# A recurrent-memory transformer with mixers on one Trainium2 core: the last mixer chunk in another order, with unread matmuls in its waits

## Chip, cores and metric

The kernel runs on one core of a Trainium2 chip, in one launch. The metric is the device time of that launch in microseconds (us); lower is better.

## What is computed

Four layers in a row on x of 2048 rows by 640: attention with a recurrent memory (A), a mixer with an MLP (B), and both again with the same weights. Cut to what matters:

```python
# A: 64 segments of 32 rows; 8 memory rows go in front of each and come out of it
for s in range(n_seg):
    h = concatenate([mem, x[s*32:(s+1)*32]])               # 40 rows
    q, k, v = h @ Wq, h @ Wk, h @ Wv                       # 32 heads of 192
    p = softmax(where(mask, q @ k.T * scale, -1e9))
    o = (p @ v) @ Wo
    mem, out = o[:8], o[8:]
# B
h = gelu(layernorm(x) @ w1)
h = concat(h[:, 0:160] one row later, h[:, 160:320] one row earlier,
           h[:, 320:480] two rows later, h[:, 480:640] two rows earlier)
x1 = x + h @ w2
return x1 + gelu(layernorm(x1) @ w3) @ w4
# all
x = x + A(layernorm(x)); x = x + B(layernorm(x)); x = x + A(layernorm(x)); x = x + B(layernorm(x))
```

## The kernel before

**Two lanes.** The first A layer and the second run side by side as two lanes, the second five segments behind the first (`LAG`). `attention_step(t)` does segment t of lane 0 and segment t - 5 of lane 1 in one go, with both lanes' 40 rows side by side (`N` is 80 columns, or 40 where only one lane has a segment: the first five steps and the last five). There are 69 steps. The 32 heads are eight groups of four; for each pair of groups `proj_pair` multiplies with Wk, Wq and Wv, partly from weights that stay in SBUF and partly from a ring of eight streamed tiles (`wst`), and `attend` does scores, softmax, values and Wo for one group. The result goes to `yTB` (L696).

**Chunks.** The mixer runs on 64 rows of both lanes at a time: `chunk(c)` and `chunk_end(c)`. Every second step carries one chunk among its matmuls, from its own ring (`wstB`) and its own two psum banks (pool B). `chunk` transposes `yTB` back to rows (psx), adds the residual (L847, xw), takes the layer norm (`ln_ops`, `apply_ln`; the inverse root is a `pow` on GpSimd, L721), transposes the result (psv), copies it to SBUF (`vT`, L896) and multiplies with w1 (L918). Because the mixer needs rows that come later, there is a look-ahead: a second row tile `lnx` with four rows beyond the chunk and the first layer norm's rows for coming segments. It has its own transposes (psl), add (L851), statistics (L874), root (L881), normalisation (L887, which writes into the same buffer `vb` as the chunk's own, so that the transposes of `vb` come after it) and copy (L900). `gelu` is four operations: square on ScalarE, polynomial on VectorE, tanh on ScalarE, product on VectorE, here in up to nine pieces because the four column quarters are shifted by one or two rows (L765). Then w2 (L963), a residual add (L969), a layer norm, w3 in three parts of five, five and two blocks of 128 columns (L998), GELU, and in `chunk_end` w4 (L1024), the last add (L1030) and the store (L1042), which GpSimd issues.

**The last chunk.** The last of 34 chunks, `last`, has only rows of lane 1 and comes after the last step, with nothing beside it. It puts its two halves of rows into the two lanes' places, so the rows at the seam are copied inside `hTB` by seven small VectorE copies (L947). Its psum tiles come from pool A's six banks, its GELU buffers lie over the resident Wv (`own`), and its weights were loaded during the last step over weights that are no longer needed (`homes`).

**What sets the order.** Nothing is issued as written. Every operation is given to a planner with an engine, an estimated length, a due time and the buffers that it reads and writes (`add`); `Plan.place` then runs a list schedule: of the operations that could start about now on an engine, the one with the earliest due time. The queues of the engines are issued in that order; a load that the planner held back for its pace gets a wait on an earlier matmul (`paced`, L1119 to L1125). So a changed estimate can change the order elsewhere. The due times of the last chunk are squeezed by `LAST_PACE`:

```python
        D = lambda x: base + x * STEP * (LAST_PACE if last else 1.0)
        PB = "A" if last else "B"
```

Of the kernel before, what the change touches and what calls it, by code (L numbers as in the profile page):

```python
# [21 lines left out]
HG = 4  # L22
# [7 lines left out]
OT_BUFS = 8  # L30
LAT = 0.12
# [39 lines left out]
class Op:  # L71
    __slots__ = ("e", "d", "due", "fn", "n", "succ", "ready", "slots", "start", "end", "dma", "i", "margin",
                 "paced", "last")


class Plan:
# [8 lines left out]
    def add(self, e, d, due, fn, r=(), w=(), a=(), dma=0, queue=None, margin=0.0):  # L85
# [6 lines left out]
        preds = set()  # L92
# [31 lines left out]
    def place(self):  # L124
# [27 lines left out]
        def est(o, t):  # L152
            s = max(t, o.ready)
            need = {}
            for b in o.slots:
                if b.slot is None:
                    need[b.cls] = need.get(b.cls, 0) + 1
            for c, n in need.items():
                fs = self.free_slots[c]
                if len(fs) < n:  # L160
                    return None
                s = max(s, fs[n - 1][0])
            if o.e == "SP":
                s = max(s, srv - ahead(o))
            return s
# [6 lines left out]
        while left:  # L172
# [29 lines left out]
            o.paced = e == "SP" and s <= srv - ahead(o) + 1e-9  # L202
# [38 lines left out]
def kernel(  # L241
# [87 lines left out]
    mask_b = ctile([L1, L1], bf16, "mask_b")  # L329
    nc.gpsimd.memset(mask_b[:], 0.0)  # L330
    keep(mask_b, L1, M, L1, -M, 1, -1, NEG)
    keep(mask_b, L1, M, L1, -M, 1, 0, 0.0)
# [11 lines left out]
    qT = qTw[:].rearrange("p (c n) -> p c n", c=GC)  # L344
    vFw = ctile([P, GC * NS], bf16, "vF")
    vF = vFw[:].rearrange("p (c n) -> p c n", c=GC)
    kT = [ctile([P, 8, NS], bf16, f"kT{i}") for i in range(2)]
    Vt = [ctile([NS, 2 * VP], bf16, f"V{i}") for i in range(2)]
# [23 lines left out]
    for i in range(2):  # L372
        nc.gpsimd.memset(kT[i][:], 0.0)
    for i in range(2):
        nc.vector.memset(Vt[i][:], 0.0)
    nc.gpsimd.memset(yTB[:], 0.0)
    nc.vector.memset(qTw[:], 0.0)
    nc.vector.memset(vFw[:], 0.0)
    nc.vector.memset(Pmw[:], 0.0)
# [131 lines left out]
    def attention_step(t):  # L511
# [4 lines left out]
        maskt = mask2[:] if both else (mask_a if 0 in ln else mask_b[:])  # L516
# [8 lines left out]
        def proj_pair(pr):  # L525
            s0 = base + sl * 2 * pr
            for kind, off in (("k", 0.0), ("q", 0.2), ("v", 0.5)):
                wbs, wv = load_pair(kind, pr, s0 + off * 2 * sl, LEAD_A)
                for j in range(2):
                    g = 2 * pr + j  # L530
                    G = t * NG + g
                    due = s0 + (off + 0.1 * j) * 2 * sl
# [3 lines left out]
                    for kcs in [range(0, nres)] + [range(kc, kc + 1) for kc in range(nres, KC)]:  # L536
                        def fn(op, pq=pq, wv=wv, j=j, kcs=kcs):
                            o = T(pq)
                            for cc in range(GC):
                                for kc in kcs:  # L540
                                    nc.tensor.matmul(out=o[:, cc, 0:N],  # L541
                                                     lhsT=wv(kc, GW * j + cc * P, GW * j + (cc + 1) * P),
                                                     rhs=h[:, kc, c0:c0 + N], start=(kc == 0 and cc == 0),
                                                     stop=(kc == KC - 1), skip_group_check=True)
                        wb = wbs[0] if kcs[0] == 0 else wbs[1 + kcs[0] - nres]
                        add("PE", mm_us(N, k=GC * len(kcs)), due + 0.01 * kcs[0], fn, r=(wb, *hk), a=(pq,))
                    if kind == "q":
                        q = qT

                        def fq(op, pq=pq, q=q):  # L550
                            nc.scalar.copy(out=q[:, :, 0:N], in_=T(pq)[:, :, 0:N])  # L551
                        add("ACT", act_us(GC * N), due, fq, r=(pq,), w=(B("qT"),))
                    elif kind == "k":
                        k_ = kT[G % 2]

                        def fk(op, pq=pq, k_=k_):
                            p4 = T(pq)[:].rearrange("p (h c) n -> p h c n", h=2)
                            k4 = k_[:].rearrange("p (h c) n -> p h c n", h=2)
                            nc.vector.tensor_copy(out=k4[:, :, 0::3, 0:N], in_=p4[:, :, 0::2, 0:N])  # L559
                        add("DVE", dve_us(4 * N), due, fk, r=(pq,), w=(B("kT", G % 2, 0),))  # L560
                        for part, (r0, r1, jj) in enumerate(((0, 64, 1), (64, P, 2))):
                            def fk2(op, pq=pq, k_=k_, r0=r0, r1=r1, jj=jj):
                                p4 = T(pq)[:].rearrange("p (h c) n -> p h c n", h=2)
                                k4 = k_[:].rearrange("p (h c) n -> p h c n", h=2)
                                nc.vector.tensor_copy(out=k4[r0:r1, :, jj, 0:N], in_=p4[r0:r1, :, 1, 0:N])  # L565
                            add("DVE", dve_us(2 * N), due, fk2, r=(pq,), w=(B("kT", G % 2, 1 + part),))
                    else:
                        vf, V_ = vF, Vt[G % 2]

                        def fvf(op, pq=pq, vf=vf):  # L570
                            nc.scalar.copy(out=vf[:, :, 0:N], in_=T(pq)[:, :, 0:N])  # L571
# [3 lines left out]
                        def fvt(op, pvt=pvt, vf=vf):  # L575
# [6 lines left out]
                        for hf in range(2):  # L582
                            def fe(op, pvt=pvt, V_=V_, hf=hf):
                                src = T(pvt)[0:N, GWH * hf:GWH * (hf + 1)].rearrange("n (a b) -> n a b", a=2)
                                v0 = hf * (VP - 64)
                                dst = V_[0:N, v0:v0 + 512].rearrange("n (a b) -> n a b", a=2)[:, :, 64 * hf:64 * hf + Dh]
# [5 lines left out]
                                w=(B("V", G % 2, hf),))  # L592

        def attend(g):
            G = t * NG + g
            s0 = base + sl * g
            q, k_, V_ = qT, kT[G % 2], Vt[G % 2]
# [3 lines left out]
            def fs(op):  # L601
                o = T(pss)
                seq = [(0, 1, 0, 0), (1, 1, 2, 3), (2, 1, 3, 4), (3, 1, 5, 7), (0, 2, 1, 1), (2, 2, 4, 5)]
                for n_, (i, w_, c, j) in enumerate(seq):
                    m_ = wide(c, GC - 1)
                    nc.tensor.matmul(out=o[0:m_, i * N:(i + w_) * N].rearrange("p (a b) -> p a b", a=w_),  # L606
                                     lhsT=qTw[:, c * NS:c * NS + m_], rhs=k_[:, j:j + w_, 0:N],
                                     start=(n_ == 0), stop=(n_ == len(seq) - 1), skip_group_check=True)
            add("PE", mm_us(N, N, 4) + mm_us(2 * N, N, 2), hi - 4, fs,
                r=(B("qT"), B("kT", G % 2, 0), B("kT", G % 2, 1), B("kT", G % 2, 2)), w=(pss,))  # L610
# [4 lines left out]
            def f1(op):  # L615
                o = T(pss)[0:N, 0:HG * N].rearrange("p (a b) -> p a b", a=HG)
                nc.vector.tensor_tensor_reduce(out=o, in0=o, in1=maskt.unsqueeze(1).to_broadcast([N, HG, N]),  # L617
                                               scale=-scale, scalar=3.0e38, op0=ALU.add, op1=ALU.min,
                                               accum_out=sm_[0:N, 0:1])
            add("DVE", dve_us(HG * N) + 0.02, hi - 4, f1, r=(pss,), w=(pss, smk))  # L620

            def f2(op):
                o = T(pss)[0:N, 0:HG * N].rearrange("p (a b) -> p a b", a=HG)
                nc.scalar.activation(out=Pb[0:N, :, 0:N], in_=o, func=ACT.Exp, bias=sm_[0:N, 0:1], scale=-1.0)  # L624
            add("ACT", act_us(HG * N) + 0.09, hi - 4, f2, r=(pss, smk), w=(Pk,))

            def f3(op):
                nc.vector.tensor_reduce(out=sm_[0:N, 2:2 + HG], in_=Pb[0:N, :, 0:N], axis=AX.X, op=ALU.add)  # L628
                nc.vector.reciprocal(out=sm_[0:N, 6:6 + HG], in_=sm_[0:N, 2:2 + HG])
                nc.vector.tensor_tensor(out=Pb[0:N, :, 0:N], in0=Pb[0:N, :, 0:N],  # L630
                                        in1=sm_[0:N, 6:6 + HG].unsqueeze(2).to_broadcast([N, HG, N]), op=ALU.mult)
# [529 lines left out]
```

## Time and profile before

| | |
|---|---|
| three runs, us | 3530.97, 3534.40, 3536.71; median 3534.4 |
| profiled execution, us | 3528.87, of which the profile's span 3527.2 |
| mean granted TensorE clock | 0.98 |
| busy: TensorE / VectorE / ScalarE / GpSimd | 94% / 70% / 43% / 7% |

By stretches of the span (start and end in us; in each row, after the length, the busy time of TensorE, of its weight loads, of VectorE, ScalarE and GpSimd, with the number of instructions; then the granted TensorE clock, the share of the DMA engines' time, and GB/s):

```profile
0.00:56.00 56.00, 35.17 (x750) 31.32 (x751) 19.74 (x79) 13.04 (x37) 6.85 (x23) 1.00 0.99 373
```
```profile
290.00:3261.00 2971.00, 2895.40 (x72649) 2832.60 (x72646) 2192.79 (x6399) 1349.38 (x3079) 215.00 (x416) 1.00 0.89 306
```
```profile
3483.80:3527.20 43.40, 17.00 (x144) 13.38 (x144) 17.07 (x54) 6.90 (x17) 3.62 (x6) 0.65 0.18 58
```

The first row is the opening, which loads the weights; the second the steps with two lanes; the third the last chunk. A row's busy time is read against its length: an engine near the length is a bound of that stretch, and where none is near, a chain of waits across engines sets the time. The granted clock is the share of TensorE's full speed that the hardware allowed; the records have it at 1.0 or 0.5, so a mean between them says for how long it was halved.

### The profile page before, as it was taken

The page shows a single profiled execution, that of the slowest core. Times are in us where ns is not written, and L with a number is a line of the kernel's source. Part 1 is how long each engine was busy: PE and PEld are TensorE (multiplying, and loading weights), DVE is VectorE, ACT ScalarE, POOL GpSimd, SP SyncE. Part 2 cuts the span into 40 slices and gives each one's busy share as a digit, 9 for nine tenths or more (in the row PEclk, how much of TensorE's full clock was granted, in tenths as well). Part 3 has the DMA queues.
Part 4 walks back from the last instruction along what each step waited for, and adds up shares of the span by engine and source line. Part 5 has one row for each costly group of instructions (what it writes and reads, how often), then busy time and mean ns, then how long its engine had stood idle before and what let it go on. Part 6 is the DMA issues. An engine that isn't in the chain of part 4 may idle for free.

```text
span 3527.2 us, 188048 instructions
## 1 busy us (share of the span) xinstructions
PE 3322.3 (94%) x84559; PEld 3231.6 (92%) x84559; DVE 2469.2 (70%) x7436; ACT 1520.6 (43%) x3569; POOL 247.1 (7%) x488
## 2 busy tenths in 40 slices
PE   5889999999999999999999999999999999999886
PEld 5879999999999999999999999999999999999775
DVE  2557777777777777777777777777777777777554
ACT  1334444444444444444444444444444444444332
POOL 0000000000000000000000000000000000000000
PEclk8899999999999999999999999999999999999897
DMA  9999898889888988898889888998889888988995
GB/s 374 304 306 317 301 324 298 294 297 316 301 307 299 315 300 299 309 321 303 302 301 327 306 295 298 316 310 303 312 305 319 298 299 301 319 300 303 307 315 176
DMA packets 497753, 1075.27 MB, mean 305 GB/s; under 512 B 49455, under 2 KB 216893, under 8 KB 496945
## 3 DMA queue, kind: packets, MB, share of 16 engines
q1 hardware_dynamic: 489712, 1050.11, 86.2%
q8 instruction: 661, 10.83, 1.2%
q0 software_dynamic: 7232, 13.13, 1.1%
q14 instruction: 148, 1.20, 0.1%
HBM read 1057.79 MB, written 5.24 MB: 301 GB/s over the span
## 4 chain that ended last, share of the span: by engine, by line
PE 88%; DMA 5%; issue 4%; DVE 1%; ACT 1%; SPq 1%; POOL 0%; POOLq 0%; DVEq 0%; ACTq 0%
PE psy L670 16%; PE psq L541 15%; PE psv L541 15%; PE psk L541 15%; PE pvt L579 5%; PE pso L653 4%; PE pss L606 4%; PE psh L998 3%; PE y L1024 3%; PE pst L639 2%; DMA wst<-in_A_Wq_dram 2%; PE psh L918 1%; DMA wst<-in_A_Wk_dram 1%; PE hs L963 1%; DMA wst<-in_A_Wv_dram 1%
## 5 line engine op out<-in xcount | busy, mean ns | idle before, releaser
L541 PEld LDWEIGHTS <-wst 128*128 128x128 bf16 x25668 | 1031.2, 100 | 43.1 <-issue 25.0
L670 PE MATMUL psy<-oT,wo 128*128 128x80 bf16 (+1 forms) x16560 | 689.8, 199 | 32.1 <-issue 19.4
L670 PEld LDWEIGHTS <-wo 128*128 128x128 bf16 x16560 | 626.3, 100 | 41.0 <-issue 29.2
L551 ACT CAST qT<-psq 128x480 bf16<-128x480 f32 (+1 forms) x552 | 292.6, 530 | 639.9 <-PE psq L541 638.6
L541 PE MATMUL psq<-hT,wst 128*128 128x80 bf16 (+1 forms) x9936 | 467.9, 199 | 19.1 <-issue 11.1
L659 DVE CAST oT<-pso 128x480 bf16<-128x480 f32 (+1 forms) x552 | 341.2, 618 | 167.2 <-PE pso L653 161.6
L541 PE MATMUL psv<-hT,wv 128*128 128x80 bf16 (+1 forms) x9936 | 434.6, 199 | 21.1 <-issue 15.9
L541 PE MATMUL psk<-hT,wst 128*128 128x80 bf16 (+1 forms) x9108 | 428.0, 199 | 11.0 <-issue 7.9
L541 PEld LDWEIGHTS <-wv 128*128 128x128 bf16 x9936 | 386.6, 100 | 28.9 <-issue 18.3
L644 ACT COPY PT<-pst 80x320 bf16<-80x320 bf16 (+1 forms) x552 | 221.9, 402 | 440.2 <-PE pst L639 433.8
L590 ACT COPY V<-pvt 80x384 bf16<-80x384 bf16 (+1 forms) x552 | 261.7, 474 | 328.5 <-PE pvt L579 301.1
L541 PE MATMUL psk<-hT,wk 128*128 128x80 bf16 (+1 forms) x7452 | 348.8, 199 | 19.5 <-ACT hT L688 10.8
L565 DVE CAST kT<-psk 64x160 bf16<-64x160 f32 (+1 forms) x1104 | 336.7, 305 | 9.7
L624 ACT ACTIVATE Pm<-pss,sm 80x320 bf16<-80x320 f32 (+1 forms) x552 | 279.7, 507 | 135.9 <-DVE sm L617 135.8
L571 ACT CAST vF<-psv 128x480 bf16<-128x480 f32 (+1 forms) x552 | 290.0, 525 | 102.0 <-PE psv L541 95.7
L541 PE MATMUL psq<-hT,wq 128*128 128x80 bf16 (+1 forms) x6624 | 320.2, 199 | 11.7 <-issue 6.6
L541 PE MATMUL psv<-hT,wst 128*128 128x80 bf16 (+1 forms) x6624 | 322.4, 199 | 7.7 <-issue 6.6
L541 PEld LDWEIGHTS <-wk 128*128 128x128 bf16 x7452 | 299.2, 100 | 26.8 <-issue 26.1
L588 DVE COPY V<-pvt 80x384 bf16<-80x384 bf16 (+1 forms) x552 | 188.1, 350 | 182.3 <-PE pvt L579 107.8
L617 DVE CUSTOM_DVE_ANT_1 pss<-pss,mask 80x320 f32<-80x320 f32 (+1 forms) x512 | 240.9, 485 | 104.7 <-PE pss L606 84.3
L559 DVE CAST kT<-psk 128x320 bf16<-128x320 f32 (+1 forms) x552 | 254.6, 461 | 69.6 <-PE psk L541 63.2
L628 DVE TENSOR_REDUCE sm<-Pm 80x4 f32<-80x320 bf16 (+1 forms) x552 | 248.9, 451 | 57.3 <-ACT Pm L624 52.2
(130 smaller groups left out, 4425.0 us busy)
## 6 DMA issues: line engine op xcount, KB each, us to landing
wst<-in_A_Wq_dram SPq DMA_DIRECT2D x828, 384.0 KB, 5.3
wst<-in_A_Wk_dram SPq DMA_DIRECT2D x759, 384.0 KB, 5.3
wst<-in_A_Wv_dram SPq DMA_DIRECT2D x552, 384.0 KB, 5.4
wstB<-in_B_w_dram SPq DMA_DIRECT2D x495, 320.0 KB, 5.0
wstB<-in_B_w_dram SPq DMA_DIRECT2D x132, 160.0 KB, 4.9
wo<-in_A_Wo_dram SPq DMA_DIRECT2D x8, 960.0 KB, 12.8
wv<-in_A_Wv_dram SPq DMA_DIRECT2D x4, 1152.0 KB, 11.9
wq<-in_A_Wq_dram SPq DMA_DIRECT2D x4, 768.0 KB, 11.7
```

Of the source, the lines that this page charges most:

```text
L541: nc.tensor.matmul(out=o[:, cc, 0:N], lhsT=wv(kc, GW * j + cc * P, GW * j + (cc + 1) * P), rhs=h[:, kc, c0:c0 + N], start=(kc == 0 and cc ...
L551: nc.scalar.copy(out=q[:, :, 0:N], in_=T(pq)[:, :, 0:N])
L559: nc.vector.tensor_copy(out=k4[:, :, 0::3, 0:N], in_=p4[:, :, 0::2, 0:N])
L565: nc.vector.tensor_copy(out=k4[r0:r1, :, jj, 0:N], in_=p4[r0:r1, :, 1, 0:N])
L571: nc.scalar.copy(out=vf[:, :, 0:N], in_=T(pq)[:, :, 0:N])
L590: nc.scalar.copy(out=dst, in_=src)
L617: nc.vector.tensor_tensor_reduce(out=o, in0=o, in1=maskt.unsqueeze(1).to_broadcast([N, HG, N]), scale=-scale, scalar=3.0e38, op0=ALU.add, ...
L624: nc.scalar.activation(out=Pb[0:N, :, 0:N], in_=o, func=ACT.Exp, bias=sm_[0:N, 0:1], scale=-1.0)
L628: nc.vector.tensor_reduce(out=sm_[0:N, 2:2 + HG], in_=Pb[0:N, :, 0:N], axis=AX.X, op=ALU.add)
L644: nc.scalar.copy(out=Pt[:, :, 0:N], in_=T(pst)[0:NS, :, 0:N])
L659: nc.vector.tensor_copy(out=o_[:, :, 0:N], in_=T(pso)[:, :, 0:N])
L670: nc.tensor.matmul(out=o[:, m, c0:c0 + N], lhsT=wo[:, cc, m * P:(m + 1) * P], rhs=o_[:, cc, 0:N], start=st, stop=True, skip_group_check=True)
```

## The change

In the last chunk:

- *No look-ahead.* Its transposes, add, statistics, root, normalisation and copy go, and so do the loads of `lnx` for it. The two columns that it supplied are copied from the chunk's own transposes, and the others set to zero by GpSimd.
- *Column halves.* The copy of the transposes to `vT` is split in a ScalarE copy of three column blocks and a VectorE copy of two (`halves`). The add after w2 is done by halves of the columns, each followed by its statistics (`parted`). The outputs are stored by column halves, from the queues of ScalarE and SP instead of GpSimd's.
- *Row-block groups.* w2 runs in two groups of blocks (three and two), w3 in four units of three blocks, each with its own GELU, and w4 in four groups of three, where each group waits only for its own blocks. Of the seven seam copies six go to ScalarE.
- *Unread matmuls.* `warm` puts matmuls of 128x512 into a psum bank of pool B that nothing reads, 26 in all, each group after an operation of the chain (the new `after` of `add`, which becomes a wait).

In all chunks, `ln_ops` leaves out the column that only the first norm needs, and its estimate is shorter. In the one-lane steps of the end, lane 1's columns keep their places (40 to 79) in the small buffers, `mask_b` is a part of `mask2`, and `hT` and `oT` are set to zero at the start. `ONE`, `HALVES`, `KT_BUFS` and `VT_BUFS` have the values at which they change nothing.

```diff
+WARM = (2, 4, 2, 1, 1, 1, 1, 6, 1, 1, 2, 1, 1)
...
+    for o_ in oT:
+        nc.gpsimd.memset(o_[:], 0.0)
...
+    for i in range(4):
+        nc.vector.memset(hT[i][:], 0.0)
...
         def f1(op):
-            for c in range(2):
+            for c in () if parted else range(2):
                 nc.vector.bn_stats(out=st[0:rows, 6 * c:6 * c + 6], in_=srcv[:, c, :])
...
+            if n == 2:
                 nc.vector.tensor_scalar(out=st[0:rows, 15:16], in0=st[0:rows, 13:14], scalar1=1.0 + EPS,
                                         scalar2=EPS * EPS, op0=ALU.mult, op1=ALU.add)
-        add("DVE", 1.37, due, f1, r=(srck,), w=(stk,))
+        o1 = add("DVE", (0.5 if parted else 1.3) + 0.07 * (n - 1), due, f1, r=(srck,), w=(stk,))
...
+    def warm(n, due, *after):
+        if not held:
+            held.append(ps("B", [P, 512], f32, "busy"))
+        wo = resident[("o", 0)][1]
+
+        def fwarm(op):
+            for i in range(n):
+                nc.tensor.matmul(out=T(held[0])[:], lhsT=ident[:, :], rhs=wo[:, 0, 0:512], start=True, stop=True)
+        add("PE", mm_us(512, k=n), due, fwarm, a=(held[0],), after=after)
...
-        add("DVE", 1.42, D(0.07), f1, r=(B("lnx", "l"), B("lnx", "x")), w=(s2k,))
+        if not last:
+            add("DVE", 1.42, D(0.07), f1, r=(B("lnx", "l"), B("lnx", "x")), w=(s2k,))
...
+        def halves(pt, due, ahead=False):
+            def fa(op):
+                nc.scalar.copy(out=vT[:, 0:3, 0:XB], in_=T(pt)[:, 0:3, :])
+            add("ACT", act_us(3 * XB), due, fa, r=(pt,), w=(vTk,))
+
+            def fd(op):
+                nc.vector.tensor_copy(out=vT[:, 3:KC, 0:XB], in_=T(pt)[:, 3:KC, :])
+            add("DVE", dve_us(2 * XB), due, fd, r=(pt,), w=(B("vTd"),))
+            if ahead:
+                def fn(op):
+                    nc.scalar.copy(out=vT[:, :, XB + 1:XB + 4:2], in_=T(pt)[:, :, 0:4:2])
+                add("ACT", act_us(KC * 2), due, fn, r=(pt,), w=(B("vTn"),))
...
+            if last:
+                for n, x in zip(WARM[5:8] if i == 0 else WARM[8:9], os_[0:3] if i == 0 else os_[3:4]):
+                    warm(n, D(0.38), x)
...
+        for u, (n0, n1) in enumerate(((0, 3), (3, 5))) if last else ():
+            for k in range(2):
+                def fw(op, k=k, n0=n0, n1=n1):
+                    for n in range(n0, n1):
+                        lhsT = hTB[:, n, 0:TOK, :].rearrange("p w l -> p (w l)")
+                        nc.tensor.matmul(out=T(hs[k])[:], lhsT=lhsT, rhs=got[n][1]()[:, got[n][2], HC * k:HC * (k + 1)],
+                                         start=(n == 0), stop=(n == 4))
...
         for k in range(2):
             def fs(op, k=k):
                 cs = slice(HC * k, HC * (k + 1))
                 nc.vector.scalar_tensor_tensor(out=uw[:, cs], in0=T(hs[k])[:], scalar=0.5, in1=uw[:, cs],
                                                op0=ALU.mult, op1=ALU.add)
-            add("DVE", dve_us(HC), D(0.5), fs, r=(hs[k],), w=(uk,))
+                if last:
+                    nc.vector.bn_stats(out=st3[:, 6 * k:6 * k + 6], in_=uw[:, cs])
...
+        for u in range(4) if last else ():
+            n0 = 3 * u
+            pz2 = ps(PB, [P, 3, XB], f32, "psh2")
+
+            def fw(op, n0=n0, pz2=pz2):
+                for kc in range(KC):
+                    for n in range(n0, n0 + 3):
+                        _, wv, j, i = w3got[n, kc]
+                        nc.tensor.matmul(out=T(pz2)[:, n - n0, :], lhsT=wv()[:, j, i * P:(i + 1) * P],
+                                         rhs=vT[:, kc, 0:XB], start=(kc == 0 and n == n0), stop=(kc == KC - 1),
+                                         skip_group_check=True)
...
+            gelu(pz2, 3, due, [(0, P, 0, 3, h2T[:, n0:n0 + 3, :])], (B("h2T", 0, u),), (uk,), own=2 + u)
...
+        for u, (n0, n1) in enumerate(((0, 3), (3, 6), (6, 9), (9, FC))) if last else ():
...
+                add("PE", mm_us(HC, k=n1 - n0), D(1.3 + 0.06 * u), fw,
+                    r=(*(got[n][0] for n in range(n0, n1)), B("h2T", 0, u)),
+                    w=() if u else (y2[k],), a=(y2[k],) if u else ())
...
+            for lane in range(2) if last else ():
+                w0 = rows_of(c, lane)
+                b = min(TOK, S - w0)
+
+                def fst(op, lane=lane, b=b, w0=w0, cs=slice(HC * k, HC * (k + 1))):
+                    (nc.scalar if lane else nc.sync).dma_start(out=outd[w0:w0 + b, cs], in_=xo[lane:2 * b:2, cs])
+                add("ACT" if lane else "SP", 0.4, D(1.6), fst, r=(B("xh", k),), dma=b * HC * 2)
...
+        for x in o.after:
+            tc.add_manual_dep(nc.cur_bb.bb.instructions[k], x.last.name, dep, reason="after")
```

## The prediction

> **What bounds the kernel now.** First the page, then busy time by stretches, then the chain of waits for the last 45 us, because the change touches little else.
>
> ```profile
> span 3527.2 us, 188048 instructions
> ```
>
> By stretches, TensorE is busy 2895 of the 2971 us between 290 and 3261: the steps with two lanes are bound by TensorE, and nothing of their matmul work changes. The last chunk is different. From the last eviction of the attention (yTB, L696, which ends at 3483.81; I call this moment F) to the end are 43.4 us, in which TensorE is busy for 17.0 and transfers run for a fifth of the time. There the bound is a chain across the engines. The chain of waits, cut to that stretch (start, length, piece):
>
> ```profile
> 3484.95 0.49 DVE h2u L851
> ...
> 3488.97 0.45 DVE vbg L887
> ...
> 3491.04 2.84 PE psh L918 x25
> ...
> 3494.22 9.10 issue
> ...
> 3506.30 4.83 PE psh L998 x48
> ...
> 3516.60 0.58 POOL out_dram L1042
> 3517.18 0.56 POOLq L1156
> ```
>
> Two pieces of the look-ahead (L851, L887) stand in the chain; so does a "9.10 issue", which the timeline resolves into GELU pieces on VectorE, the matmuls of w2 and a layer norm. And the chain ends at 3517.74, 9.4 us before the span does. What fills these 9.4 us is seen in the instructions of the closing line (shortest/median/longest ns) and in SP's own waits:
>
> ```profile
> L1156 POOLq DRAIN  x3: 46/102/9346, 3517.0 to 3526.9; - x3
> ```
> ```profile
> SPq L1156 <- PEq L1156: 7.7, 2, 7.2
> ```
>
> The two output transfers land 1.9 us after issue, about 3519.1; SP then waits 7.2 us more. GpSimd's drain, which starts at 3517.0 while it issues those transfers, takes 9.35 us, and only then the closing barrier runs (3526.4 to 3527.2). This is the largest single thing in the stretch.
>
> **The change part by part, counted from F.** Before-times are from the timeline of the tail; "cold" and "full" are granted clocks of 0.5 and 1.0.
>
> A. *Look-ahead out.* From F to the transposes of vb (3489.47) now 5.66. Without L851 (0.52 with its gap), without the statistics of lnx that hold back L727 (VectorE free at 3488.09, POOL's root ready at 3487.63), and without L887 with its wait for the second root (3488.25 + 0.69), there remain: transposes of yTB and add to 1.11, statistics up to POOL's start 1.46 after their own start (L707 at 3485.46, POOL at 3486.92), POOL 0.71, normalise 0.45, gaps 0.1: 3.83. Gain **1.83**. What is late next is POOL's root.
>
> B. *Evacuation in column halves.* Now one ScalarE copy of 640 (0.69) and one of 20 (0.18), 0.82 from the start of one to the first psh matmul. The halves look parallel, but in the compiled order of the changed kernel VectorE's half waits for ScalarE's half, and ScalarE's two zero-edge columns wait for VectorE's. The trace has this pattern already, for two engines reading one psum tile:
>
> ```profile
> 3480.40 0.47 ACT L590 COPY V<-pvt 40x384 bf16<-40x384 bf16 x1 [0.60 <-PE pvt L579]
> ...
> 3480.91 0.35 DVE L588 COPY V<-pvt 40x384 bf16<-40x384 bf16 x1
> ```
>
> VectorE starts 0.04 after ScalarE ends. The Trainium skill (PSUM — Partial Sum Buffer, "PSUM bank collisions raise a hardware error") says that a scheduler orders any two instructions of different engines on one bank, reads too. It speaks against this part: parallel halves would be 0.47 + 0.05 + 0.18, about 0.7 (gain 0.1); one after the other 0.47 + 0.30 (256 columns, estimated below the 0.35 of 384) + 0.18 + gaps 0.15 = 1.10, a loss of **0.28**. I take the loss. The transposes before it hand over 0.75 after their start cold (3489.47 to 3490.22) and 0.48 at full clock (psx, 3483.95 to 3484.43), so full clock takes 0.27 off each of the two. At the second use (L983) the first matmul needs ScalarE's half alone, 0.47 for 0.69: gain **0.23**, and nine matmuls (0.96 cold) cover VectorE's half.
>
> C. *Matmuls of w1*, unchanged: 2.64 from first matmul to first GELU instruction, cold; at full clock 23 x 0.059 (L998 late: 15 in 0.88) + 0.1 = 1.45. Between 0 and **-1.2**.
>
> D. *Shift copies and w2 in row blocks.* GELU up to its last step is unchanged (1.74). From the last step's start (3495.42) to the residual add (3501.09) 5.67. The nine pieces (2.90) stay; the seven copies of L947 (1.16) shrink to one on VectorE and six on ScalarE, beside the pieces. The first block of w2 could start at the sixth piece, but an unread matmul that waits for the ninth stands ahead of it in TensorE's queue. So 2.95 + one unread matmul (0.43 cold, 0.22 full; estimated from 512 columns at the pace of 320) + 8 matmuls (0.26 each cold by L963, 0.139 full by L1024) + 0.15: 5.6 cold, 4.4 full. Gain **0.05 to 1.25**.
>
> E. *Statistics by halves*: add and statistics alternate with a wait each, so the pairs (0.89 + 0.88 overlapped) become about 2.0: +0.3; one tensor_scalar (0.07) and one column of the root (0.71 mean against 0.55 for the one-column form) less. Net **+0.1**.
>
> G. *w3 in four units of three blocks, w4 in four groups.* First matmul to final add 9.12 now, cold until about 3510.6, full after. In the change the last unit ends as before (3506.30 + 5.4 with the same warm-up), its GELU chain (0.43 + 0.49 + 0.45 + 0.49 and gaps, 2.1) runs beside 18 matmuls of w4, and 21 matmuls (2.9) lead to the add: 8.4. With full clock throughout, ScalarE's and VectorE's 1.0 per unit set it: 6.75. Gain **0.7 to 2.4**.
>
> H. *Output from SP and ScalarE instead of POOL, by column halves.* Second add ends 0.89 after the first begins, issue 0.1 later, landing 2.1 (between 1.9 of POOL's output and 2.3 of SP's first load; ScalarE issues no transfer in this trace: 0 to 1.5 more), SP's closing waits 0.27, barrier 0.75: 4.1 instead of 11.75. POOL's last work is then the root in E, some 13 us earlier; even a drain of 9.35 begun there is over before the outputs land, and the drain at the program's start, with no transfer before it, took 0.18. Gain **7.65**; if the drain stayed behind the end, 0.
>
> *The unread matmuls (26).* Their worth is the difference of the two ends above: -10.1 if all is cold, -14.7 if all is full (with 0.27 twice for the transposes). The trace by windows of 3.41 us, on the grid at which its clock changes (second number PE busy, PEclk third from the end):
>
> ```profile
> 3435.39:3438.81 3.42, 2.53 (x58) 2.10 (x55) 2.04 (x8) 1.81 (x7) 0.00 (x0) 1.00 1.02 346
> 3438.81:3442.22 3.41, 2.63 (x77) 2.45 (x73) 0.90 (x3) 0.35 (x2) 0.00 (x0) 0.50 0.52 197
> ...
> 3490.01:3493.42 3.41, 2.84 (x30) 2.72 (x29) 0.00 (x0) 0.77 (x2) 0.00 (x0) 0.50 0.19 67
> ...
> 3507.07:3510.49 3.42, 3.42 (x35) 3.42 (x33) 0.89 (x2) 1.19 (x3) 0.00 (x0) 0.50 0.02 5
> 3510.49:3513.90 3.41, 3.12 (x37) 2.37 (x35) 3.10 (x8) 2.65 (x8) 0.00 (x0) 1.00 0.00 0
> ```
>
> A window 74% busy lost the clock for the next; one 83% busy did not win it back; a full one did. The Trainium skill (TensorE: Matmul & The Clock Gate, "Why this matters for your kernels") asks only for no idle gap above about 3 us: the longest gap left is some 1.7, so by the rule the clock stays full, -14.7. By the row it doesn't: at full clock I count 2.3 us of PE work in the first window after F (67%, undecided), then 1.3 to 2.3 (39 to 66%) until w3. I take the row: full through B, half of C, then cold, with the refilled windows warming w3 a little earlier. -1.83 + 0.1 - 0.6 - 0.2 + 0.1 - 0.23 - 1.0 - 7.65 = **-11.3**.
>
> *Outside the tail.* The start gains eight memsets on POOL (480 columns, 0.43 each by the 0.59 step of yTB's 660) and loses mask_b's three (0.45), ahead of the first root: it moves from 7.04 to about 10. VectorE's four memsets of hT (0.9) are covered by that. First projection +3.0. It is hidden: in every slice of 2 us from 4 to 60 the DMA share is 0.97 to 1.07, and TensorE waits for loads at 12.6 and, 1.8 us, at 19.4. Cost 0, uncovered 3.0. Every chunk loses one tensor_scalar and a column of the root, off the chain. The planner's shorter estimate for it reorders a few matmul groups in steps 2 to 6 and 64 to 66; same work: 0, between -4 and +4.
>
> The sum stands against the profiled execution: 3528.87 (span 3527.2), so 3517.6. The three runs have median 3534.4, 5.5 above it and 5.7 apart; the tail is a fixed stretch, so I subtract from the median: **3523**.
>
> **Rivals.** (1) Forecast, drain off the path and clock lost: 3523, chance 0.62. (2) The filler holds the clock, as the rule has it: 3534.4 - 14.7 = 3520; against it the 74% window; 0.15. (3) The drain belongs to the program's end and not to POOL's transfers: H gains only what the others leave, -3.7: 3531, no measurable change; for it, that no wait names it; against it the 0.18; 0.09. (4) The tail gains, but the reordered steps give most of it back (4 to 18 us): 3523 to 3541; 0.08. (5) Slower: the clock in the one-lane steps. From 56 to 272 and 3275 to 3500 single windows of 3.41 us run at half clock, 33 in all, chosen by gaps as small as the 26% above. A reordering that opens gaps costs up to 1.7 us for each window more; with 11.3 gained it decides for "slower" from about 11 windows more: 3542 or above; 0.06. For it, the start's 3 us and the moved groups; against it, that the work and its loads are the same.
>
> **How the numbers follow.** A difference under 0.2% (7.1 us) can't be told from none. Faster by more: (1) and (2) = 0.77. Same: (3) and (4) = 0.17. Slower 0.06. The range reaches from (2), less the spread of the runs, to (3): 3516 to 3530.5.
>
> **What would show it.** The span ends within 5 us of the last add, with GpSimd's drain short or early (H). The transposes of vb start 3.8 us after F (A). VectorE's half begins when ScalarE's ends (B). Granted clock in the tail near 0.7, with half-clock windows between F + 4 and w3; near 1.0 would be rival 2. The stretch up to F should keep its 3483.8 within 4 us; if it doesn't, (4) or (5) holds.

## The result, and the profile after

Six runs of the changed kernel: 3502.92, 3520.94, 3525.91, 3523.02, 3520.07, 3507.04 us, median 3520.5. The kernel before, six runs beside them: median 3535.6. The ratio is 0.9947 with a 95% interval of 0.9922 to 0.9972: 15 us faster at the medians, 19 by the ratio, which compares means, and between 10 and 28 by the interval.

The profiled execution is the shortest of the six (3502.92 us).

```profile
span 3501.2 us, 187978 instructions
```

Its span is 26.0 us below that of before, and that is not the size of the change. The last yTB eviction ends at F = 3471.38 instead of 3483.81, so 12.4 us are gained before the last chunk begins. The experiments below show that this part is the spread of the body (all steps before F) from execution to execution. From F to the end are 29.8 us instead of 43.4: **13.6 us** are the change's own.

Where the 13.6 us lie, each piece measured from the start of one instruction to the start of the next named one (us):

| piece | before | after | difference | forecast |
|---|---|---|---|---|
| A: F to the transposes of vb | 5.66 | 4.12 | -1.54 | -1.83 |
| B: transposes to w1's first matmul | 1.57 | 1.62 | +0.05 | +0.1 |
| C: w1 and GELU up to its last step | 4.38 | 3.21 | -1.17 | -0.6 |
| D: last GELU step to the residual add | 5.68 | 4.26 | -1.42 | -0.2 |
| E: add to the second transposes | 3.67 | 3.71 | +0.04 | +0.1 |
| second evacuation, to w3's first matmul | 1.54 | 1.08 | -0.46 | -0.23 |
| G: w3 and w4, to the final add | 9.11 | 6.84 | -2.27 | -1.0 |
| H: final add to the end of the span | 11.75 | 4.97 | -6.78 | -7.65 |
| sum | 43.36 | 29.81 | -13.55 | -11.3 |

The chain of waits of the changed kernel around the first evacuation and at its end (start, length, piece):

```profile
3475.51 0.47 PE psv L753 x5
3475.97 0.02 issue
3476.00 0.49 ACT hTB L940
3476.48 0.02 issue
3476.51 0.30 DVE hTB L944
...
3476.89 0.19 ACT hTB L948
3477.08 0.04 issue
3477.12 1.57 PE psh L980 x25
...
3496.22 0.90 DVE vbg L1162 x2
```

VectorE's half (L944) stands in the chain behind ScalarE's (L940): the halves are read one after the other, as step B said. At the end the chain goes on to the stores; the closing line's instructions on GpSimd (shortest/median/longest in ns, first and last start) and SP's waits read:

```profile
L1303 POOLq DRAIN  x3: 46/93/9176, 3487.0 to 3500.9; - x3
```
```profile
SPq L1303 <- DMA out_dram<-vbg: 1.5, 2, 1.0
SPq L1303 <- PEq L1303: 0.7, 2, 0.5
```

GpSimd's drain still takes 9.18 us. But it begins at 3487.0, with the root that is GpSimd's last work, and is over at 3496.2, when the final add begins. SP now waits for the output transfers (1.5 us in all) and not for 7.2 us of another engine.

The clock did not go the way of the forecast. By windows of 3.41 us on the grid at which it changes (second number TensorE's busy time, third from the end its clock):

```profile
3473.36:3476.77 3.41, 2.45 (x13) 0.78 (x12) 1.80 (x7) 0.48 (x1) 0.72 (x1) 1.00 1.05 368
3476.77:3480.19 3.42, 2.34 (x27) 1.57 (x26) 0.92 (x3) 1.43 (x5) 0.22 (x1) 1.00 0.16 56
3480.19:3483.60 3.41, 1.99 (x10) 0.89 (x11) 2.56 (x10) 1.50 (x8) 0.00 (x0) 1.00 0.00 0
3483.60:3487.01 3.41, 1.22 (x10) 0.76 (x8) 2.28 (x7) 0.00 (x0) 0.00 (x0) 1.00 0.00 0
3487.01:3490.43 3.42, 2.72 (x28) 1.65 (x29) 1.09 (x3) 0.50 (x2) 0.72 (x1) 1.00 0.02 5
```

Up to the final add only the stretch from F to F + 2.0 is at half clock; from F to the end of the span it is 0.7 of a window, where before had 8.9. Windows in which TensorE is busy 58% and 36% of the time (the latter about 42% with one matmul whose record is missing) were followed by full clock, although before lost the clock after one of 74%.

### The profile page after: what moved, and what is told of

The parts are those of the page before. It is cut to its first block, busy times and chain, and to the rows that moved or that the text cites. A ratio compares the mean times of both kernels' runs of the same rounds, so it can differ in the third digit from the quotient of the medians.

```text
span 3501.2 us, 187978 instructions
## 1 busy us (share of the span) xinstructions
PE 3319.2 (95%) x84571; PEld 3225.6 (92%) x84573; DVE 2466.0 (70%) x7360; ACT 1519.5 (43%) x3573; POOL 235.3 (7%) x489
## 3 DMA queue, kind: packets, MB, share of 16 engines
q14 instruction: 145, 1.19, 0.1%
## 4 chain that ended last, share of the span: by engine, by line
PE 90%; DMA 4%; issue 3%; DVE 2%; ACT 1%; SPq 0%; POOL 0%; POOLq 0%; DVEq 0%; ACTq 0%
PE psy L692 16%; PE psq L553 16%; PE psk L553 16%; PE psv L553 15%; PE pvt L591 5%; PE pso L665 4%; PE pss L618 4%; PE psh L1102 3%; PE y L1147 3%; PE pst L651 2%; DMA wst<-in_A_Wk_dram 2%; PE psh L980 1%; PE hs L1039 1%; DMA wst<-in_A_Wq_dram 1%; PE psv L753 1%
## 5 line engine op out<-in xcount | busy, mean ns | idle before, releaser
L602 ACT COPY V<-pvt 80x384 bf16<-80x384 bf16 x552 | 261.5, 474 | 329.8 <-PE pvt L591 301.1
L629 DVE CUSTOM_DVE_ANT_1 pss<-pss,mask 80x320 f32<-80x320 f32 (+2 forms) x552 | 253.8, 474 | 143.0 <-PE pss L618 136.7
L636 ACT ACTIVATE Pm<-pss,sm 80x320 bf16<-80x320 f32 (+2 forms) x552 | 279.3, 506 | 136.0 <-DVE sm L629 135.8
L600 DVE COPY V<-pvt 80x384 bf16<-80x384 bf16 x552 | 188.5, 350 | 174.6 <-PE pvt L591 102.4
L591 PE MATMUL pvt<-ident,vF 128*128 128x128 bf16 x3312 | 282.3, 222 | 10.1 <-issue 7.3
```

Of the source, the lines that this page charges most:

```text
L591: nc.tensor.transpose(out=o[0:w_, c * P:(c + 1) * P], in_=vFw[:, c * NS:c * NS + w_], identity=ident[:, :])
L602: nc.scalar.copy(out=dst, in_=src)
L636: nc.scalar.activation(out=Pb[0:NR, :, c0:c0 + N], in_=o, func=ACT.Exp, bias=sm_[0:NR, 0:1], scale=-1.0)
```

## The experiments

All tails below are read like the table: F and the span's end of each kernel's own profiled execution, one for each kernel. The late memset, the narrow filler, the matmul ahead of w2 and the one copy were executed only once. Run times are worth less here, because the body spreads: the 30 runs of the kernel before that stood beside the first four experiments go from 3524.9 to 3551.0.

### The body: its order alone, and the tail alone

Two kernels split the change between them. The first is the changed kernel with the body's old order:

```diff
-        o1 = add("DVE", (0.5 if parted else 1.3) + 0.07 * (n - 1), due, f1, r=(srck,), w=(stk,))
+        o1 = add("DVE", 0.5 if parted else 1.37, due, f1, r=(srck,), w=(stk,))
-            ln_ops(xo, XB, st_, s4k, B("xo"), D(1.5), 1)
+            ln_ops(xo, XB, st_, s4k, B("xo"), D(1.5), 2)
...
-    for o_ in oT:
-        nc.gpsimd.memset(o_[:], 0.0)
-    for i in range(4):
-        nc.vector.memset(hT[i][:], 0.0)
```

> The changed kernel with the planner's old estimate for the layer norm statistics (1.37 us), their second scalar step and second root column in every chunk but the last, and without the twelve added start-up memsets: TensorE's order of matmuls up to the last chunk is then that of the kernel before. Theory 1 (the gain is the tail's and the body gives nothing that is regular): tail 29 to 30.5 us, F within 3 us of 3484 or spread as the changed kernel's was, median gain 13 to 15 us. Theory 2 (the reordered groups gave the 12.4 us by which F came earlier in the changed kernel's profiled run, or a part of it): F near 3484, no run below 3515, and a median 2 us or more above that of the changed kernel.

The second is the kernel before with these edits the other way round:

> The kernel before with the complement: the shorter estimate of the statistics, one scalar step and one root column in every chunk, and the twelve start-up memsets, so that TensorE's order up to the last chunk is exactly that of the changed kernel; the last chunk is as before. Theory 1 (the body gives nothing regular): median within 2 us of the kernel before, tail 43 to 44 us. Theory 2 (the reordering gives time): median 4 to 12 us below the kernel before, F at 3471 to 3480.

Measured: the tail on the old order has ratio 0.9951 (0.9932 to 0.9971), median 3520.5, tail 31.21, F 3479.6. The order alone has ratio 0.9993 (0.9979 to 1.0007), median 3537.8 against 3537.2, tail 42.66, F 3495.7. The body gives nothing that can be measured, and the tail gives all within the noise. One prediction of theory 1 missed: a tail of 31.21 lies above its 29 to 30.5 span, because one more window ran at half clock (see below).

F over the ten profiled executions, by the order of TensorE's groups in the body:

| order | F (us) | mean | half-clock windows before 300 us |
|---|---|---|---|
| old | 3483.8, 3492.5, 3479.6 | 3485.3 | 21, 20, 21 |
| new | 3471.4, 3494.8, 3495.7, 3484.6, 3488.7, 3479.5, 3475.3 | 3484.3 | 28 to 31 |

The changed kernel's own 3471.4 is the lowest of a spread of 24 us. By the time of each step's last eviction, the difference between two executions drifts by a few us up and down all the way; against before, the changed kernel's grew by 10.6 us between steps 11 and 26 and then stayed between 10 and 15. What makes it drift was not traced. The last column shows what the reordering does do: seven to eleven more windows at half clock, in each of its seven profiled executions, nearly all between 20 and 56 us. It costs nothing that can be measured: there the DMA engines are the limit (share of their time 1.03 in the changed kernel and before, with the clock at 0.50 and 1.00), and the time of the order alone is that of before. The added memsets of the start cost nothing either: as forecast, the first transposes of the first layer norm start 3 us later (11.43 for 8.42), but the first step's last eviction ends at 88.7, not later than the 89.3 of before.

### The stores alone

The kernel before with the last chunk's stores by column halves from SP and ScalarE, and nothing else:

```diff
+            for lane in range(2) if last else ():
...
+                    (nc.scalar if lane else nc.sync).dma_start(out=outd[w0:w0 + b, cs], in_=xo[lane:2 * b:2, cs])
+                add("ACT" if lane else "SP", 0.4, D(1.6), fst, r=(B("xh", k),), dma=b * HC * 2)
```

> The kernel before with one part of the change alone: the last residual add's two column halves are stored by SP and ScalarE, each when its half is done, and GpSimd issues no output transfer at the end. Theory 1 (GpSimd's drain of 9.2 us begins when GpSimd's own last work is done, here the root that ends at 3504.2, and so lies beside the w3 and w4 matmuls): from the start of the last add to the end of the span 11.75 falls to about 5, the tail from 43.4 to about 36.6, and the run is 6.5 to 7 us faster. Theory 2 (the drain belongs to the end of the whole program, or begins only when all engines are done): no gain, within 1 us. Theory 3 (the forecast's size: the drain also becomes short): the same gain as theory 1, but a drain of under 1 us in the instructions of the closing line.

Measured: ratio 0.9980 (0.9964 to 0.9995), that is 7 us with 2 to 13 by the interval; tail 37.22. From the final add's start to the end 5.09 instead of 11.75: 6.66 of it is H. The rest of the tail is 0.5 longer (0.16 before the first transposes and 0.37 from w3 to the final add), with its half-clock windows lying elsewhere. GpSimd's drain, in the instructions of this kernel's closing line:

```profile
L1168 POOLq DRAIN  x3: 46/102/9411, 3512.2 to 3529.5; - x3
```

It is as long as ever, 9.41 us, but runs from F + 19.7 to F + 29.1, before the final add begins at F + 32.1. So theory 1 holds and theory 3, the forecast's short drain, does not. The drain is 9.17 to 9.41 us in all ten profiled executions. The 9.4 us of before were not the price of the last transfers, but of GpSimd being the engine that worked last: in the eight executions without them GpSimd's last transfer was issued more than 50 us before the end of the attention, and the drain is as long. Why it takes 9 us at all stays open. GpSimd's drain at the start of the program takes 0.18 to 0.19 us in every trace; between the two lie over 220 transfers and all of GpSimd's work, and no run leaves these out.

### A GpSimd instruction at the end: a miss, and what it leaves open

```diff
+            def fp(op):
+                nc.gpsimd.memset(hist[:], 0.0)
+            add("POOL", 0.2, D(1.6), fp, r=(B("xh", 1),), w=(B("hist"),))
```

> The changed kernel with one small GpSimd memset (of hist, which nothing reads any more) that waits for the last add; the stores stay on SP and ScalarE, and GpSimd issues no transfer at the end. Theory 1 (GpSimd's drain takes 9.2 us at the end of its own program, whether or not it has issued a transfer lately): the drain begins some 0.3 us after the last add (F + 26) instead of F + 15.6, and the span ends about 10.5 us after the last add's end instead of 4.1 to 4.3: tail 35.5 to 36.5. Theory 2 (the drain waits for GpSimd's transfers, as the forecast had it): the drain is short and the tail stays at 29.5 to 31.5.

Measured: tail 30.40, drain 9.25 us from F + 16.15. That looks like theory 2, but the memset ran at F + 16.85, right behind the root. The planner's note of a dependence sets its place in the order; a wait comes only from the data, and hist shares none with the final add. So this run says nothing of a late GpSimd instruction. A version that writes columns that the final add reads, and so must wait for it, was not run: whether a late instruction without a transfer brings the 9.2 us back to the end stays open. It does give the changed tail a second time.

### Without the unread matmuls

```diff
-WARM = (2, 4, 2, 1, 1, 1, 1, 6, 1, 1, 2, 1, 1)
+WARM = (0,) * 13
```

> The changed kernel without its 26 unread matmuls; everything else is as changed. The changed kernel's own tail, from the end of the last yTB eviction (F) to the end of the span, was 29.8 us with one window at half clock. Theory 1 (the unread matmuls hold the clock, because they leave no idle gap as long as a window): without them TensorE has gaps of about 3.3 to 4 us (between the two sets of transposes, before w2, before the second transposes), the clock goes to half in most windows from F + 5 to the w3 matmuls, and the tail is about 33 to 34.5 us, less up to 1 us because w2's first block no longer has an unread matmul ahead of it. Theory 2 (the dense matmuls of 128 and 512 columns that the chain has anyway hold it): the tail stays at about 29 to 30 us with clock 1.0 nearly throughout, and the filler is worth nothing.

The tuple sums to 24 unread matmuls, not 26, and the two pages agree: 84,573 weight loads with them and 84,549 without.

Measured: tail 33.01, at half clock from F to F + 23.65; ratio 0.9960 (0.9944 to 0.9976). The outcome is that of theory 1; its reason, the gap, is tested in the next section. Against the 29.81 of the changed kernel the filler is worth 3.2 us, against the 31.21 of the same tail on the old order 1.8; run times, whose intervals overlap (0.9922 to 0.9972 with filler), cannot tell. The 3.2 are made of a gain and a loss. At half clock, w1 and the GELU take 4.38 instead of 3.21, the second evacuation 1.34 instead of 1.08, and w3 to the final add 8.74 instead of 6.84. The first transposes to w1's first matmul, at half clock too, take 1.87 instead of 1.62. But w2's first matmul starts at F + 10.95 instead of F + 11.92, since no unread matmul stands ahead of it, and D is 3.85 cold against 4.26 with full clock.

This run also splits the change: without filler the tail is 10.35 below that of before, 6.76 of it H, 1.82 D and 1.54 A. The forecast's sum for a tail that is cold throughout was 10.1.

### What holds the clock: columns, busy time or gaps

For each window of the traces, three numbers can be counted from the matmul records: the columns that the matmuls starting in it stream (a matmul of 128x512 streams 512), the busy share and the longest idle gap. A limit on each, set for each of the two clocks as well as it can be, sorts the windows of the ten traces (20 to 280 us and after 3250; 1,068 that ran at full clock and 418 at half) by the clock of the next window with so many left on the wrong side:

| measure | limit at full clock, wrong | limit at half clock, wrong | wrong of 1,486 |
|---|---|---|---|
| columns in the window | 3,200: 33 | 3,240: 12 | 45 |
| busy share | 0.58: 73 | 0.89: 34 | 107 |
| longest gap | 1.43 us: 99 | 0.28 us: 44 | 143 |

Only columns have one limit for both states. Weighting each matmul's columns with the share of the 128 input rows that it uses sorts better still: counted over the same stretches (1,505 windows), one weighted limit of 3,056 for both clocks leaves 25 on the wrong side, one unweighted limit of 3,200 leaves 42. No run separates these two counts; every matmul of the changed kernel's tail uses all 128 rows, so for the tail they are the same. All this is correlation; the test takes columns away and leaves most of the busy time. Each unread matmul of 512 columns becomes four of 32:

```diff
-            for i in range(n):
-                nc.tensor.matmul(out=T(held[0])[:], lhsT=ident[:, :], rhs=wo[:, 0, 0:512], start=True, stop=True)
+            for i in range(4 * n):
+                nc.tensor.matmul(out=T(held[0])[:, 0:32], lhsT=ident[:, :], rhs=wo[:, 0, 0:32], start=True, stop=True)
```

> The changed kernel with each unread matmul of 512 columns replaced by four of 32 columns: the same stationary operand loaded four times (0.05 us each at full clock), so nearly the same busy time at the same places, a quarter of the columns. Theory 1 (columns: a window of 3.41 us keeps or gets the full clock when at least about 3,300 columns were streamed in it, which is what sorts 858 of 885 windows of the six traces so far): with a quarter of the filler's columns the windows after F fall to 1,300 to 3,200 columns, and the clock is lost from about F + 3 to the w3 matmuls as without filler; tail about 33. Theory 2 (busy share or the length of the idle gap decides): the clock is held as in the changed kernel, tail 29.5 to 31.

Windows of this kernel after F = 3484.60, numbers as in the windows above:

```profile
3486.39:3489.80 3.41, 1.74 (x30) 1.34 (x27) 1.72 (x7) 0.33 (x1) 0.72 (x1) 0.50 1.07 366
...
3493.22:3496.63 3.41, 1.46 (x34) 1.00 (x32) 2.42 (x8) 2.55 (x9) 0.22 (x1) 1.00 0.00 0
3496.63:3500.04 3.41, 2.32 (x13) 1.40 (x14) 1.03 (x5) 0.19 (x1) 0.00 (x0) 0.50 0.00 0
```

The matmuls that start in the first of these windows stream 1,216 columns; those of the second, at full clock, 1,024, after which the clock is lost. In the changed kernel the first and third window of the view above have 11 and 10 matmuls that start in them, with 3,712 and 4,544 columns, and keep it. The longest gap from F to w3 is 2.03 us here and 2.2 in the changed kernel by the records (1.76 with the missing one), and in the window of 1,024 columns no gap is above 0.95, so gaps don't separate them. From F to the end there are 7.2 half-clock windows and a tail of **34.69**, longer even than without filler: the narrow matmuls do as little for the clock as none, and still stand ahead of w2 (D is 5.20 here, 3.85 without filler). The busy time was not kept exactly (1.46 against 1.99 in the second row), so this run alone speaks against gaps more sharply than against busy share. Against busy share speaks the table, and that a window 43% busy lost the clock here, where the changed kernel's window of 36% (42% with the missing record) kept it, a thin margin. That last window is itself the worst misfit of columns: 2,240 by the records that start in it, about 3,100 with one unread matmul whose record is missing (its weight load is there) and one that starts 0.03 before it. The limit is known to some hundreds of columns, no better.

The tail on the body's old order shows the limit from the other side. In its windows

```profile
3493.40:3496.82 3.42, 1.67 (x9) 0.59 (x10) 2.53 (x7) 0.00 (x0) 0.73 (x1) 1.00 0.00 0
3496.82:3500.23 3.41, 3.22 (x30) 2.73 (x27) 0.56 (x2) 0.97 (x2) 0.00 (x0) 0.50 0.02 5
```

the first has 2,688 columns (the four unread matmuls around the second statistics and the five transposes) and the next runs at half clock. The fifth unread matmul of this stretch starts at 3496.83, in the next window. Two other runs have the same stretch with all five in one window (3,200 columns, one of the five by its weight load alone, its matmul's record missing), and keep the clock: the late memset from F + 15.1 and the one copy from F + 14.0. The tail on the old order is the changed kernel's own tail, 1.4 us longer, because the grid lies otherwise over the same work: whether the weakest stretch, between w2 and the second transposes, fills a window is chance.

### The matmul ahead of w2

```diff
-WARM = (2, 4, 2, 1, 1, 1, 1, 6, 1, 1, 2, 1, 1)
+WARM = (2, 4, 2, 1, 1, 1, 1, 6, 0, 1, 2, 1, 1)
```

> The changed kernel without the one unread matmul that waits for the ninth GELU piece and stands ahead of w2's first block in TensorE's queue. Theory 1 (that matmul holds w2 back for nothing): w2's first matmul at F + 11.0 instead of 11.9, and the residual add at F + 12.4 to 12.7 instead of 13.2, the tail 0.5 to 0.8 shorter if the clock is the same. Theory 2 (the last GELU piece of the second half sets the add anyway): the first matmul is earlier but the add stays at F + 13.2.

In the changed kernel (F = 3471.38) the unread matmul waits for the ninth GELU piece, and w2 (L1048) comes behind it:

```profile
3483.08 0.39 PE L799 MATMUL busy<-wo,ident 128*128 128x512 bf16 x1 [1.32 <-DVE hTB L784]
3483.30 0.43 PE L1048 MATMUL hs<-wq,hTB 128*128 128x320 bf16 x2
```

The timeline of this kernel (F = 3479.50):

```profile
3489.71 0.44 PE L1050 MATMUL hs<-wq,hTB 128*128 128x320 bf16 x2
...
3491.76 0.49 DVE L1058 SCALAR_TENSOR_TENSOR h2u<-hs,h2u 128x320 bf16<-128x320 f32 x1 [0.54 <-PE hs L1050]
```

w2 starts at F + 10.2, earlier than the 11.0 expected and before the sixth piece begins (F + 10.4), and the add at F + 12.26 instead of F + 13.21: theory 1, and 0.95 us instead of 0.5 to 0.8. The tail is 29.96 all the same, because the stretch behind it now has 1,856 columns by the records (one of 512 more has none) and the next window, F + 15.6 to F + 19.0, is at half clock: the second evacuation is 1.34 for 1.08, w3 to the final add 7.64 for 6.84. The gain was taken back by the clock.

### One copy for the first evacuation

```diff
-            halves(ps2, D(0.1), True)
+            add("ACT", act_us(KC * XB), D(0.1), fe, r=(ps2,), w=(vTk,))
+            def fn1(op):
+                nc.scalar.copy(out=vT[:, :, XB + 1:XB + 4:2], in_=T(ps2)[:, :, 0:4:2])
+            add("ACT", act_us(KC * 2), D(0.1), fn1, r=(ps2,), w=(B("vTn"),))
```

> The changed kernel with the first evacuation of the transposes as one ScalarE copy of all 640 columns and the two edge columns behind it, instead of column halves on ScalarE and VectorE. Theory 1 (the halves run one after the other and cost 0.28 us, as the forecast had it): from the transposes to w1's first matmul 1.3 to 1.4 us instead of 1.61. Theory 2 (the shorter VectorE half makes up for the second start): 1.55 to 1.65, no difference.

ScalarE in the timeline of this kernel:

```profile
3479.96 0.69 ACT L952 COPY hTB<-psv 128x640 bf16<-128x640 bf16 x1 [7.60 <-PE psv L753]
3480.55 0.19 ACT L963 COPY hTB<-psv 128x10 bf16<-128x10 bf16 x1
```

From the transposes to w1's first matmul 1.30 instead of 1.62: theory 1. Two copies on one engine even overlap a little (the second starts 0.59 after the first), while the halves on two engines wait for each other twice. Tail 29.58, the shortest of all; its distance of 0.2 to the changed kernel's is less than the 1.4 that the grid alone makes, so the gain is read from the piece and not from the tail.

A combination of the last two, with more wide unread matmuls around the second statistics, is what these runs point to. It was not run; the sum of the two gains, 0.95 + 0.31, would be less than the spread of the body.

## Why the prediction was right, and where it was not

The forecast, 3523 with a gain of 11.3, stands beside a median of 3520.5 and a gain of 13.6 in the tail. The direction and the main terms held; the case that happened is not the likeliest one of the text but rival 2. That the median lies within a microsecond of rival 2's 3520 is luck: the six runs go from 3502.9 to 3525.9.

**The failed step: "I take the row".** The forecast weighed a window 74% busy that lost the clock against the rule of the Trainium skill (TensorE: Matmul & The Clock Gate, "Why this matters for your kernels") that asks only for no idle gap above some 3 us, and chose the row. The row's number was a busy share of short matmuls (31 of its 51 stream 40 columns); the windows to be forecast were full of matmuls of 512, 320 and 128. Counted in columns, the row's window had 3,416, some 200 on the wrong side of the limit that all the traces give (weighted with rows it has 3,056, at the weighted limit), and the one at 83% that did not win the clock back 3,216, at it; the changed kernel's windows at 58 to 72% have 3,712 to 4,544, clearly above it. Busy share could not be carried from one kind of matmul to another. The rule gave the right answer for this kernel, but the narrow filler, with no gap above 2.03 us, lost the clock, so by these runs the gap is not what decides.

That one step explains most of the sizes of C, D, the second evacuation and G: together 5.32 where 2.03 was booked. The full-clock ends that the text had worked out, 1.19 for C, 1.25 for D, 2.37 for G and 0.50 for the second evacuation with its handover, make 5.31; that the sums agree to 0.01 is luck, since D came out 0.17 better and G 0.1 worse. The narrow filler shows the same pieces mostly at half clock: C 4.38, D 5.20, the second evacuation 1.33 and G 8.98, against 3.21, 4.26, 1.08 and 6.84 at full clock, which is 4.5 us.

**A** was short by 0.3, and 0.25 of it is the first transposes, which run cold, since the one-lane matmuls before F had already lost the clock; the forecast had it full through B. Before, the same five took 0.44:

```profile
3471.53 0.69 PE L868 MATMUL psx<-ident,yTB 128*128 128x128 bf16 x5 [0.53 <-DVE yTB L718]
```

**B** was right in mechanism and size: the halves are serial, and one copy is 0.31 shorter where 0.28 was said.

**D** named the unread matmul in front of w2. It costs 0.95, and the 0.22 to 0.43 that the text gave it were its own length alone: the greater part is that w2 waits for the ninth piece when its first matmuls could start before the sixth. The sum of D did not suffer, because it put all of w2 behind the ninth piece: 4.4 at full clock where 4.26 was measured. What the text lacked is the price of leaving that matmul there.

**E** was right: +0.04 for +0.1.

**H** was right in what leaves the path and mis-sized by 0.87: 4.97 where 4.1 was said. What was sized too low is the issue, by these rows of the changed kernel's timeline:

```profile
3496.75 1.20 ACTq L1174 DMA_DIRECT2D out_dram<-vbg  x2
3496.78 1.39 SPq L1174 DMA_DIRECT2D out_dram<-vbg  x2
```

Each engine issues its two transfers one behind the other, 0.6 to 0.7 us each, so that the last is issued at 3498.17, 1.05 after the final add ends, where 0.1 was booked. The drain did not become short, but was early, and the text had covered either. Rival 3 was right that the drain does not hang on the last transfers, and wrong that it belongs to the program's end: it comes at the end of GpSimd's own work.

**The body**: more windows of half clock came, seven to eleven, but nearly all between 20 and 56 us, where the transfers are the limit, and not in the one-lane steps of rival 5; no cost could be measured. F is spread by 24 us, so that the "3483.8 within 4 us" asked of it could not have told anything. One profile of before could not show this spread; its three times (3531.0 to 3536.7) showed a quarter of it.

## What to carry to other kernels

Look at what the program's last microseconds wait for: an engine whose closing drain takes 9 us should do its last work early, and the final stores should come from engines with a short one. By these runs unread matmuls hold the clock by the columns they stream rather than by the time they keep TensorE busy, so use wide ones, and let none wait for an event later than the one that releases the real work standing behind it. When executions spread by more than the change is worth, compare the fixed stretch that it touches, from an event to the end, and not whole spans.

## What the runs showed of the hardware

- GpSimd's closing drain takes 9.17 to 9.41 us in every profiled execution, with or without a transfer of its own in the last 50 us; those of TensorE, VectorE and ScalarE take 1.2 to 1.5, 0.5 to 0.8 and 0.4 to 0.5. Part of each can be the wait for the engine's own last instruction (0.7 us, the root, of GpSimd's in the changed kernel).
- The granted clock of the next window of 3.41 us goes with the columns streamed in this one, with one limit near 3,200 for both clocks, 45 of 1,486 windows aside; columns weighted with the input rows in use fit as well or better. The same tail cost 29.8 or 31.2 us depending on how the grid fell on it.
- Thirty executions of the kernel before go from 3524.9 to 3551.0 us, and at F seven executions with one and the same order of TensorE's work up to there are spread by 24 us, drifting apart over the length of the body.
